# Windowed attention and a maxout feed-forward: first transfers per head half, x moved by DMA in the last three blocks, the first chunk masked by TensorE, half of the second products copied by ScalarE

## The chip, the core and the metric

The kernel runs on one NeuronCore of a Trainium2 chip. A core has TensorE (PE) for matrix products, VectorE (DVE), ScalarE (ACT) and GpSimd (POOL) for elementwise work, SyncE (SP) which here only issues transfers, and 16 DMA engines that move data between HBM and the on-chip memory SBUF. TensorE writes its products into PSUM, eight banks of 2 KB per partition, from which VectorE or ScalarE must fetch them. Each engine works through its own instructions in the order in which they were written; semaphores tie the engines together. The metric is the device time of one execution in microseconds.

## The reference

Four sequences of 768 positions, eight heads of 64, attend to the last 128 positions and to the first four (the sinks). The result, laid out as 3072 tokens of 512 features, goes through three products of which the elementwise maximum is kept, and an output product.

```python
scores = scale * np.matmul(q, k.transpose(0, 1, 3, 2))
is_sink = pos[None, :] < int(n_sink)
rel = pos[:, None] - pos[None, :]
keep = is_sink | ((rel >= 0) & (rel < int(window)))
...
a = np.exp(scores - max)
a = a / (np.sum(a, axis=-1, keepdims=True) + 1e-09)
attn = np.matmul(a, v)
...
x = attn.transpose(0, 2, 1, 3).reshape(B * S, H * D)
h = np.maximum(np.maximum(x @ w1, x @ w2), x @ w3)
out = h @ w_out
```

q, k, v are 4x8x768x64, w1 to w3 are 512x768, w_out is 768x512, all fp32 in HBM; products are made in bf16.

## The kernel before, in words

The 3072 tokens are 24 tiles of 128. Two tiles of one sequence are a chunk (12 chunks, `ch`, three to a sequence: c = 0, 1, 2), and the eight heads are taken as two halves of four (`g`). A unit is one chunk of one half: 24 units. Tiles are gathered in blocks (`BLOCKS`, L683: 2, 2, 4, 4, 4, 4, 4 tiles); a block's x goes through the feed-forward together.

**One unit** (`unit`, L382). q and k arrive by `qk_chunk` (L183): a GpSimd transfer which turns fp32 into bf16, into one of `NBUF` = 4 buffers per half. VectorE transposes them in pieces of 32x32 (L302). Scores (S, L412) are made with keys on the partitions, four heads at once in four row groups of TensorE, into `st`, which takes four of the eight PSUM banks and has one buffer only: the next unit's scores can start when this one's exps have read it. ScalarE takes the exp (E, L417), VectorE multiplies by a mask of zeros and ones (M, L424), TensorE multiplies by v, which has a column of ones for the denominator (PV, L433 and L442), VectorE divides (N, L452 and L461), TensorE transposes x (XT, L471), ScalarE copies it to `xT` (XC, L483). For c > 0 the sinks' scores are made apart (`sink_scores`) and multiplied by `vbd`, a block matrix of the sinks' v which SP fills by 16 small transfers per sequence (`sink_v`, L335).

**One block** (`block`, L548). For each of six blocks of 128 hidden features, three groups of four products (H, L562); ScalarE copies the first from PSUM to `h_sb` (L571), VectorE takes the maximum with the second and third (L573). Then for each tile six products with `wo_sb` (Y, L581), a copy by ScalarE (L588) and a store by SP (L595). H, Y, PV, XT and sink scores share the four other PSUM banks (`h_ring`).

**Loads.** `qk_first` (L162) brings q and k of chunk 0, half 0, as fp32 by SP and ScalarE, four transfers each, and ScalarE casts them (L306). GpSimd issues the rest in this order: q and k of half 1, the masks (`make_masks`), v of the first two tiles (`v_chunk`), a third of w1 to w3, the small constants `bd` and `ident`, chunk 1, two v tiles, the rest of w, chunk 2, two v tiles, `wo`. For later sequences, v comes as two large transfers (`v_batch`, L286) into one of two buffers (`vbufs`), issued between the first chunk's half 0 and half 1. Eight GpSimd transfers can be out at once.

**The order of everything** is worked out ahead of time by a list planner. Each piece of work is a `Task` with an engine, an assumed cost, the tasks it needs, a due time `want` and the buffers it takes; `arrange` (L41) picks, for each engine, among the 64 tasks due first, the one that could begin earliest. Each engine then gets its instructions in that order. `LEAD` makes a block's attention end some us before the block's turn. The planner only sets the order; on the chip each instruction waits for what it needs.

The softmax here doesn't subtract the row's maximum and nothing guards it: scores larger than these inputs give would overflow.

## Time and profile before

| | |
|---|---|
| median of 13 executions | 195.96 us (194.45 to 199.07) |
| the profiled execution | 196.5 us, of which 194.8 are the span from first to last instruction |
| instructions | 4237 |
| products H, 512 and 256 columns | L562: 345 and 144 seen, 379 and 285 ns each, 104.8 us busy |
| products Y | L581: 138 seen, 32.6 us busy |
| maxima of 128x512 from PSUM | L573: 60, 687 ns |
| masks of 128x1024 | L424: 40, 682 ns |
| exps of 128x1024 | L417: 40, 1023 ns |
| transposes of q and k | L302: 24 and 24, 633 and 626 ns |
| x to xT by ScalarE | L483: 24, 588 ns |
| HBM read and written | 25.17 MB, 6.29 MB |

The time is that of the device, the span lies inside it. Durations of one instruction are longer than the spacing in a pipelined series (two transposes of q and k start 0.46 us apart), and a few records of matmuls are missing: 489 of 504 H products are in the trace. A row of the timeline gives start, length, engine, line, operation, output and inputs, a count, and in brackets the idle time before it with what ended it.

### The profile page before, as it was taken

The page shows a single profiled execution, that of the slowest core. Times are in us where ns is not written, and L with a number is a line of the kernel's source. Part 1 is how long each engine was busy: PE and PEld are TensorE (multiplying, and loading weights), DVE is VectorE, ACT ScalarE, POOL GpSimd, SP SyncE. Part 2 cuts the span into 40 slices and gives each one's busy share as a digit, 9 for nine tenths or more (in the row PEclk, how much of TensorE's full clock was granted, in tenths as well). Part 3 has the DMA queues.
Part 4 walks back from the last instruction along what each step waited for, and adds up shares of the span by engine and source line. Part 5 has one row for each costly group of instructions (what it writes and reads, how often), then busy time and mean ns, then how long its engine had stood idle before and what let it go on. Part 6 is the DMA issues. An engine that isn't in the chain of part 4 may idle for free.

```text
span 194.8 us, 4237 instructions
## 1 busy us (share of the span) xinstructions
PE 168.3 (86%) x1659; PEld 94.7 (49%) x1680; DVE 128.8 (66%) x289; ACT 95.6 (49%) x147; POOL 55.5 (29%) x83
## 2 busy tenths in 40 slices
PE   0067988596799879999999999999999999999992
PEld 0044666265574445654445644555545556444440
DVE  4358676674999299996599953987906588035520
ACT  3253653672564616865266373827852572432222
POOL 7996758624692150257210000000000000000000
PEclk9999999999999999999999999999999999999999
DMA  5999999999999969099990022000050000230014
GB/s 110 130 155 163 195 188 176 175 140 216 137 129 137 145 67 177 25 88 179 238 140 13 3 108 111 0 0 3 0 204 15 2 3 0 108 113 0 0 54 162
DMA packets 58964, 19.52 MB, mean 100 GB/s; under 512 B 44352, under 2 KB 55616, under 8 KB 58944
## 3 DMA queue, kind: packets, MB, share of 16 engines
q0 software_dynamic: 54592, 12.40, 72.1%
q1 hardware_dynamic: 4160, 6.59, 9.5%
q10 hardware_dynamic: 192, 0.26, 0.5%
q8 instruction: 13, 0.21, 0.4%
q14 instruction: 7, 0.06, 0.1%
HBM read 25.17 MB, written 6.29 MB: 161 GB/s over the span
## 4 chain that ended last, share of the span: by engine, by line
PE 49%; DMA 28%; issue 10%; POOL 8%; SPq 2%; DVE 1%; ACT 0%; POOLq 0%; ACTq 0%
PE h L562 30%; DMA q_raw<-in_q_dram 14%; PE y L581 11%; DMA k_raw<-in_k_dram 7%; DMA v_sb<-in_v_dram 5%; PE o L442 3%; PE st L412 3%; POOL w_sb L199 3%; SPq L335 2%; PE xt L471 2%; POOL v_sb L290 2%; DMA vbd<-v_sb 1%; PE o L433 1%; POOL v_sb L194 1%; POOL q_raw L188 1%
## 5 line engine op out<-in xcount | busy, mean ns | idle before, releaser
L562 PE MATMUL h<-xT,w_sb 128*128 128x512 bf16 (+1 forms) x489 | 104.8, 351 | 5.4 <-DVE h_sb L573 3.7
L573 DVE TENSOR_TENSOR h_sb<-h,h_sb 128x512 bf16<-128x512 f32 (+1 forms) x84 | 51.2, 610 | 34.8 <-PE h L562 31.4
L562 PEld LDWEIGHTS <-w_sb 128*128 128x128 bf16 x504 | 46.1, 99 | 40.9 <-issue 4.1
L417 ACT ACTIVATE e_sb<-st 128x1024 bf16<-128x1024 f32 (+1 forms) x48 | 44.0, 952 | 17.1 <-PE st L412 16.3
L571 ACT CAST h_sb<-h 128x512 bf16<-128x512 f32 (+1 forms) x42 | 22.1, 526 | 43.7 <-PE h L562 43.5
L581 PE MATMUL y<-wo_sb,h_sb 128*128 128x512 bf16 x138 | 32.6, 379 | 2.1 <-DMA wo_sb<-in_moe_w_out_dram 1.8
L424 DVE TENSOR_TENSOR e_sb<-e_sb,mask 128x1024 bf16<-128x1024 bf16 (+1 forms) x48 | 29.7, 638 | 2.5 <-ACT e_sb L417 2.4
L412 PE MATMUL st<-qT,kT 32*128 32x128 bf16 (+1 forms) x512 | 15.4, 248 | 10.3 <-DVE kT L302 10.0
L302 DVE STREAM_TRANSPOSE qT<-q_raw 128x256 f32<-128x256 f32 x24 | 15.0, 633 | 13.5 <-DMA q_raw<-in_q_dram 13.5
L588 ACT COPY y_sb<-y 128x512 f32<-128x512 f32 x24 | 14.1, 587 | 16.4 <-PE y L581 14.0
L581 PEld LDWEIGHTS <-h_sb 128*128 128x128 bf16 x144 | 13.7, 98 | 17.0 <-issue 1.8
L461 DVE TENSOR_TENSOR x<-o,rc 128x256 bf16<-128x256 f32 x48 | 20.4, 424 | 1.8
L442 PEld LDWEIGHTS <-e_sb 128*128 128x128 bf16 x352 | 16.9, 99 | 8.2 <-DVE e_sb L424 2.5
L442 PE MATMUL o<-v_sb,e_sb 128*128 128x65 bf16 x352 | 18.9, 197 | 1.6 <-DVE e_sb L424 1.4
L483 ACT COPY xT<-xt 128x512 bf16<-128x512 bf16 x24 | 14.1, 588 | 12.5 <-PE xt L471 12.3
L188 POOL DMA_DIRECT2D k_raw<-in_k_dram x23 | 15.6, 676 | 14.0 <-DMA q_raw<-in_q_dram 7.8
L188 POOL DMA_DIRECT2D q_raw<-in_q_dram x23 | 15.9, 690 | 12.2 <-DMA q_raw<-in_q_dram 4.4
L412 PEld LDWEIGHTS <-kT 32*128 32x128 bf16 x512 | 10.2, 96 | 15.5 <-DVE kT L302 10.0
L302 DVE STREAM_TRANSPOSE kT<-k_raw 128x256 f32<-128x256 f32 x24 | 14.7, 626 | 1.2 <-DMA k_raw<-in_k_dram 1.2
L471 PE MATMUL xt<-ident,x 128*128 128x128 bf16 x96 | 12.3, 227 | 2.1 <-DVE x L461 2.1
L471 PEld LDWEIGHTS <-x 128*128 128x128 bf16 x96 | 7.6, 99 | 9.8 <-DVE x L461 4.4
L290 POOL DMA_DIRECT2D v_sb<-in_v_dram x6 | 8.6, 1442 | 12.5 <-PE st L412 10.5
(34 smaller groups left out, 48.1 us busy)
## 6 DMA issues: line engine op xcount, KB each, us to landing
out_dram<-y_sb SPq DMA_DIRECT2D x24, 256.0 KB
q_raw<-in_q_dram POOLq DMA_DIRECT2D x23, 128.0 KB, 9.9
k_raw<-in_k_dram POOLq DMA_DIRECT2D x23, 128.0 KB, 8.3
w_sb<-in_moe_w_dram POOLq DMA_DIRECT2D x9, 256.0 KB, 7.8
v_sb<-in_v_dram POOLq DMA_DIRECT2D x6, 384.0 KB, 10.8
vbd<-v_sb SPq DMA_DIRECT2D x64, 0.5 KB
v_sb<-in_v_dram POOLq DMA_DIRECT2D x6, 128.0 KB, 7.6
wo_sb<-in_moe_w_out_dram POOLq DMA_DIRECT2D x1, 768.0 KB, 9.3
```

Source lines behind the costliest of these rows:

```text
L188: nc.gpsimd.dma_start(out=raw(nm, ch, g), in_=s)
L302: nc.vector.transpose(dst, src)
L412: nc.tensor.matmul(ps[:, i, col:col + n], lhsT=kk[r, k0:k0 + 128, e], rhs=qT[r, q0:q0 + n, e], start=(e == 0), stop=(e == 1))
L417: nc.scalar.activation(st["e"][:, :, cols(tt)], st["ps"][:, :, cols(tt)], AF.Exp, scale=scale)
L424: nc.vector.tensor_tensor(out=ee, in0=ee, in1=m.unsqueeze(1).to_broadcast(list(ee.shape)), op=ALU.mult)
L442: nc.tensor.matmul(o[:, i, :], lhsT=st["e"][:, i, col:col + 128], rhs=vbufs[b % 2][:, 4 * g + i, kb, :], start=(c == 0 and n == 0), stop=( ...
L461: nc.vector.tensor_tensor(out=x, in0=o[:, :, :D], in1=rc.unsqueeze(2).to_broadcast([128, 4, D]), op=ALU.mult)
L471: nc.tensor.transpose(st["xt"][:, n, 128 * tt:128 * tt + 128], x[:, 128 * n:128 * n + 128], ident)
L562: nc.tensor.matmul(ps[:, :ntok], lhsT=w_sb[:, wi, d, fb * 128:fb * 128 + 128], rhs=xTs[blk][:, d, :ntok], start=(d == 0), stop=(d == DSUB ...
L571: nc.scalar.copy(hs, ps[:, :ntok])
L573: nc.vector.tensor_tensor(out=hs, in0=ps[:, :ntok], in1=hs, op=ALU.max)
L581: nc.tensor.matmul(ps, lhsT=box["h"][:, fb, 128 * m:128 * m + 128], rhs=wo_sb[:, fb, :], start=(fb == 0), stop=(fb == FSUB - 1))
```

## The change

- **Planner**: engines' clocks start at 0.8, 200 tasks are looked at instead of 64, and the assumed costs of loads are other ones.
- **Loads**: q of half 1 of chunk 0 comes as fp32 by SP too, with a cast by ScalarE; k of half 1 comes in four transfers by GpSimd. `NBUF` is 8, there are four v buffers, one per sequence, and v comes tile by tile for all sequences, after the q and k of both halves of its chunk.
- **Masks**: made from one triangle (`make_own`, GpSimd) by VectorE. For chunk 0 (`N_BY_PE` = 1) the mask is added before the exp: TensorE multiplies `ident` by a tile of zeros and -30000 into the score banks ahead of the scores, and VectorE's mask product falls away.
- **q's order**: q is transposed with the tokens of a tile in another order (j outside, m inside). For x that goes by TensorE, the copy to `xT` puts them back, in one copy per tile; for x that goes by DMA, the store to HBM does.
- **x by DMA** in blocks 5 to 7 (`FIRST_BY_DMA` = 5): x of both halves is gathered in `xd`, and SP issues one transposing transfer of 128x512 per tile into `xT` instead of XT and XC.
- **TWO**: in blocks 1 to 4, for hidden blocks 0, 2 and 4, ScalarE copies the second product to `h2`, and VectorE takes the maximum of two bf16 tiles in SBUF.
- **Blocks**: 2, 2, 2, 4, 4, 4, 4, 2 tiles; `LEAD` is 5.

```diff
-    clock = dict.fromkeys(engines, 0.0)
+    clock = dict.fromkeys(engines, 0.8)
...
-            for t in q[:64]:
+            for t in q[:200]:
...
+    if N_BY_PE:
+        neg = const.tile([128, 256], BF16, name="neg")
+        neg0 = const.tile([128, 384], BF16, name="neg0")
...
-    vbufs = [const.tile([128, H, 6, D + 1], BF16, name=f"v_sb{n}") for n in range(2)]
+    vbufs = [const.tile([128, H, 6, D + 1], BF16, name=f"v_sb{n}") for n in range(B)]
...
-    rate = 0.40
-
-    def load(name, mb, want, f, eng="POOL", cost=0.65, deps=(), lat=2.5):
+    rate = 0.38
+
...
-        dma_done[name] = task("DMA", mb / rate, lambda: None, deps=[t], want=want, lat=lat, name=name)
+        dma_done[name] = task("DMA", mb / (0.235 if name[0] == "v" else rate), lambda: None, deps=[t], want=want, lat=lat, name=name)
...
-    NBUF = 4
+    NBUF = 8
...
+    def qk_first(nm, src, g, e):
+
+        def f():
+            to = raw(nm, 0, g) if e is nc.gpsimd else first[nm, g]
+            for i in range(4):
+                e.dma_start(out=to[32 * i:32 * i + 32, :], in_=rows(src, 0, g)[i])
+        return f
...
+    def v_tile(b, n):
         def f():
-            s = v[0].rearrange("h (n p) d -> p n h d", p=128)
-            nc.gpsimd.dma_start(out=vbufs[0][:, :, n, :D], in_=s[:, n])
+            s = v[b].rearrange("h (n p) d -> p n h d", p=128)
+            nc.gpsimd.dma_start(out=vbufs[b][:, :, n, :D], in_=s[:, n])
...
+    load("q0.1", 0.26, -1999, qk_first("q", q, 1, nc.sync), eng="SP", cost=1.8)
...
+    def v_loads(ch):
+        b, c = divmod(ch, NC)
         for n in (2 * c, 2 * c + 1):
-            load(f"v0{n}", 0.26, nxt(), v_chunk(n), cost=0.9)
+            load(f"v{b}{n}", 0.26, nxt(), v_tile(b, n), cost=0.9)
...
+    def make_own():
+        nc.gpsimd.memset(mask[:, 128:], 1.0)
+        own = mask[:, 128:].rearrange("k (j m) -> k j m", j=8)
+        nc.gpsimd.affine_select(out=own, in_=own, compare_op=ALU.is_ge, fill=0.0,
+                                base=0, pattern=[[1, 8], [8, 16]], channel_multiplier=-1)
...
+        nc.vector.tensor_scalar(out=mask[:, :128], in0=mask[:, 128:], scalar1=-1.0, scalar2=1.0,
+                                op0=ALU.mult, op1=ALU.add)
+        nc.vector.tensor_copy(mask0[:, 0:128], mask[:, 128:256])
+        nc.vector.tensor_copy(mask0[:, 128:384], mask)
+        nc.vector.memset(mask0[0:n_sink, 0:256], 1.0)
+
+    def make_negs():
+        for m, n in ((mask, neg), (mask0, neg0)):
+            nc.vector.tensor_scalar(out=n, in0=m, scalar1=-1.0, scalar2=30000.0, op0=ALU.add, op1=ALU.mult)
...
+    load("k0.1", 0.26, nxt(), qk_first("k", k, 1, nc.gpsimd), cost=2.4)
+    for _ in range(3):
+        lanes.append(lanes[-1])
+    t_own = task("POOL", 1.8, make_own, want=nxt(), name="own")
+    t_ident = task("POOL", 0.6, make_ident, want=nxt(), name="ident")
...
+                src = raw(nm, ch, g).bitcast(F32)
+                dst = tile_T(nm, ch, g).rearrange("p s e -> p (s e)").bitcast(F32)
+                if nm == "q":
+                    dst = dst.rearrange("p (s j m) -> p j s m", s=2, j=8)
+                    src = src.rearrange("p (j s m) -> p j s m", j=8, s=2)
+                else:
+                    dst = dst.rearrange("p (m j) -> p j m", j=8)
+                    src = src.rearrange("p (j c) -> p j c", j=8)
...
+        by_pe = ch < N_BY_PE
...
+            if by_pe:
+                lo, hi = cols(tts[0]).start, cols(tts[-1]).stop
+                m = neg0[:, lo - 128:hi - 128] if c == 0 else \
+                    neg.unsqueeze(1).to_broadcast([128, len(tts), 256])
+                for i in range(4):
+                    nc.tensor.matmul(ps[:, i, lo:hi], lhsT=ident, rhs=m, start=True, stop=False,
+                                     skip_group_check=True)
...
-            src = st["xt"][:, :, 128 * tts[0]:128 * tts[0] + n]
-            nc.scalar.copy(xT_tile()[:, 2 * g:2 * g + 2, off:off + n], src)
+
+            src = st["xt"][:, :, 128 * tts[0]:128 * tts[0] + n].rearrange("p n (s j m) -> p n s m j", j=8, m=16)
+            dst = xT_tile()[:, 2 * g:2 * g + 2, off:off + n].rearrange("p n (s m j) -> p n s m j", j=8, m=16)
+            for t in range(len(tts)):
+                nc.scalar.copy(dst[:, :, t], src[:, :, t])
...
-        ms = {tt: task("DVE", 0.1 + n_e[tt] / 1880, masks(tt), deps=[es[tt], t_mask],
-                       want=w0 + (1.3 + 0.4 * tt) * dw, name=f"M{nm}{tt}") for tt in tts}
+        ms = es if by_pe else {
+            tt: task("DVE", 0.1 + n_e[tt] / 1880, masks(tt), deps=[es[tt], t_mask],
+                     want=w0 + (1.3 + 0.4 * tt) * dw, name=f"M{nm}{tt}") for tt in tts}
...
+                elif wi == 1 and fb in two:
+                    box["h2"] = ffn.tile([128, 512], BF16, name="h2", tag="h2", bufs=2)
+                    nc.scalar.copy(box["h2"][:, :ntok], ps[:, :ntok])
...
+        def both(fb):
+            def f():
+                hs = box["h"][:, fb, :ntok]
+                nc.vector.tensor_tensor(out=hs, in0=hs, in1=box["h2"][:, :ntok], op=ALU.max)
...
-                nc.sync.dma_start(out=out[r:r + 128, :], in_=box["ysb", m])
+                to = out[r:r + 128, :]
+                if blk >= FIRST_BY_DMA:
+                    to = to.rearrange("(m j) d -> j m d", j=8)
+                nc.sync.dma_start(out=to, in_=box["ysb", m])
...
-BLOCKS = [[0, 1], [2, 3], [4, 5, 6, 7], [8, 9, 10, 11], [12, 13, 14, 15], [16, 17, 18, 19], [20, 21, 22, 23]]
-TWO = ()
-LEAD = 6.0
+BLOCKS = [[0, 1], [2, 3], [4, 5], [6, 7, 8, 9], [10, 11, 12, 13], [14, 15, 16, 17], [18, 19, 20, 21], [22, 23]]
+TWO = {1: (0, 2, 4), 2: (0, 2, 4), 3: (0, 2, 4), 4: (0, 2, 4)}
+LEAD = 5.0
 N0 = 1
-N_BY_PE = 0
-FIRST_BY_DMA = 99
-XLAT = 3.0
+N_BY_PE = 1
+FIRST_BY_DMA = 5
+XLAT = 2.2
```

The transposing transfer was in the kernel before, unused, and is called now:

```python
        def xt_dma(tt):
            def f():
                o = off + 128 * (tt - tts[0])
                nc.sync.dma_start_transpose(out=xT_tile()[:, :, o:o + 128],
                                            in_=xs_tiles[ch, tt].rearrange("p h d -> p (h d)"))
            return f
```

## Prediction

> **What bounds the kernel now.** I read the page's busy rows and 40 slices first, then its chain.
>
> ```profile
> PE 168.3 (86%) x1659; PEld 94.7 (49%) x1680; DVE 128.8 (66%) x289; ACT 95.6 (49%) x147; POOL 55.5 (29%) x83
> ...
> PE   0067988596799879999999999999999999999992
> ...
> DMA  5999999999999969099990022000050000230014
> ...
> PE 49%; DMA 28%; issue 10%; POOL 8%; SPq 2%; DVE 1%; ACT 0%; POOLq 0%; ACTq 0%
> ```
>
> A slice is 4.87 us. From slice 20 (97 us) TensorE is at 9 everywhere and DMA mostly idle; before it DMA is at 9 and TensorE has 5s, 6s and 8s. So there are two regimes: an early half in which data arrives late, a later half bound by TensorE. DMA's 28% of the chain lies wholly in the first.
>
> Busy is not useful work, so I price TensorE by the steadiest rows of its chain: 47 products of 512 columns in 10.14 us, 0.216 each; 8 of 256 columns in 0.87, 0.109 each; 24 score products in 0.57 (16 in 0.46); 8 of value in 0.25; a transpose 0.055; a sink group 0.34. Before has 360+144 products of 512 columns (108.9 us), 144 of 256 (15.7), 16 score groups of 24 and 8 of 16 (12.8), 352 value products and 32 sink products at 0.11 (14.6), 96 transposes (5.3), five sink groups (1.7): **159 us** in a span of 194.8. The other 36 us are what a change can win; the timeline of TensorE shows where they are.
>
> ```profile
> 9.97 0.83 PE L412 MATMUL st<-qT,kT 32*128 32x256 bf16 x16 [9.97 <-DVE kT L302]
> ...
> 18.59 1.04 PE L412 MATMUL st<-qT,kT 32*128 32x128 bf16 x24
> ...
> 24.12 0.64 PE L412 MATMUL st<-qT,kT 32*128 32x128 bf16 x24
> ...
> 37.68 2.75 PE L581 MATMUL y<-wo_sb,h_sb 128*128 128x512 bf16 x11 [1.80 <-DMA wo_sb<-in_moe_w_out_dram]
> ...
> 49.76 0.60 PE L562 MATMUL h<-xT,w_sb 128*128 128x256 bf16 x4 [2.39 <-DVE h_sb L573]
> ...
> 58.06 2.75 PE L581 MATMUL y<-wo_sb,h_sb 128*128 128x512 bf16 x12
> ...
> 68.67 0.27 PE L433 MATMUL o<-vbd,e_sink 128*128 128x260 bf16 x1 [1.20 <-DVE h_sb L573]
> ```
>
> Counting work along the program's order: 14.8 us of it before the first output product (37.68), 30.7 before block 1's (58.06), 128.2 from there to TensorE's end at 191.25. **Loss: 22.9, then 4.5, then 5.0 us; 3.5 us of tail.** The stalls named h_sb at 49.76 and 68.67 are not the evacuation's fault: VectorE takes its instructions in order, and stood at a q or k transpose whose transfer was out.
>
> ```profile
> DVE qT L302 <- DMA q_raw<-in_q_dram: 13.5, 7, 4.1
> ```
>
> **The change, part by part.**
>
> *Loads.* Bytes stay. What moves is order. Before, batch 1's whole v (two issues, 31.5 to 34.4 us) sits between head half 0 and half 1 of chunk 3; k of half 1 is issued at 35.12 and lands 13.7 us later (48.8). After, all four q/k of a chunk come first, then two v tiles. Chunk 3's first half landed near 40.5; 0.5 MB of fp32 follows at about 0.3 MB/us (some 11 of the page's 25.2 MB are read by the time wo is in, 37.6): whole by about 42, its first v tile by 43.5. A chunk is then 1.6 MB, 5.2 us of transfer against 13 us of TensorE work (159/12). With eight raw buffers and four v buffers nothing on POOL waits for a consumer as it did for 10.5 us at 81. POOL issues 61 us in all (88 transfers at 0.67 to 0.91), spread over some 85: no bound. I take off the 2.39 us at 49.76 and, after 58.06, the stalls 1.20, 0.58 and 0.47 (68.67, 69.78, 97.60): 4.6 us.
>
> *Start.* Casts ran at 6.76 and 7.29. VectorE now takes q and k of half 0 only (two transposes, 0.46 apart), so first scores can begin near 8.6 instead of 9.97. q of half 1 comes on SP behind four issues of 0.45 (landing about 8.5), k in four POOL issues of 0.67 (same), which put v and w off by about 0.5 us; the two shorter POOL tasks give that back by the time of chunk 1. VectorE's six new mask steps, each no dearer than POOL's 0.24 to 0.39 for them now, end near 6.5, before the casts do.
>
> *First chunk masked by TensorE.* Removes four VectorE products (0.42+0.68 twice); adds eight matmuls of 384 columns. The first four run before the transposes. The second four stand in the path: the scores have one buffer, so they start only when the exps have read it. Here the rule is weighed against the row: the Trainium skill, "TensorE: Matmul & The Clock Gate", Part 1, says the clock doubles after about 3.4 us of sustained activity. By it, four would cost 4x0.16=0.64. But the timeline's 24 score products take 1.04 us at 18.59, 8.6 us after the first matmul, and 0.64 at 24.12, though the page's granted clock reads 9 throughout; activity with holes stays slow. I take 4x0.32=1.3 against 0.68 of mask saved: +0.6. Start and masks together: 1.4-0.6, first FFN product 0.8 us earlier.
>
> *Order of blocks.* Block sizes go from 2,2,4,4,4,4,4 tiles to 2,2,2,4,4,4,4,2. 256-column products take half as long, so work is the same (93.6 us both ways). What matters is the new order: the compiled TensorE order has 32 products of block 1 before the first output product, 19.6 us of work (masks 1.3 included) where before had 14.8. So **the 1.80 us for wo and the thin work around it get filled**. The feed doesn't move: chunk 2's last transposes end near 34.4 as now; then 24 FFN products, a score group and four more (2.6+0.6+0.4) put the first output product at 38.0, with 4.8 us more behind it. That is worth 4.8-1.3-0.3=3.2 us.
>
> *x by DMA in blocks 5 to 7.* Removes 40 transposes (2.2 us of TensorE) and 10 copies of 0.59 on ACT. Adds ten 128x512 transposing transfers on SP: none in the trace. The order leaves, between a block's last value products and its first FFN product, 24 output products (5.2 us) plus in two blocks a score group or more: 5.2 to 6.1 us. Lower end: SP's nearest row, SBUF to SBUF (issue 0.58, landing 2.67):
>
> ```profile
> 62.58 0.58 SPq L335
> ...
> 67.61 2.67 DMA vbd<-v_sb
> ```
>
> normalising 1.1 + two issues 1.2 + 2.7 = 5.0: no stall. Upper end: if the crossbar writes 32-byte pieces, each like those 130-byte packets (18.5 ns in the packet records), a transfer takes 4096x18.5/16 = 4.7 us, two in a row 9.4, stall about 7 us in each of three blocks. The nearest row has the same route; I take 1.0 in all. Behind the waiting SP instruction stand only stores, four y buffers deep.
>
> *Sink copies.* Batch 1's 16 vbd copies start when its first v tile lands (43.5) and take 11 us on SP, plus 2.67: 57.2. The order wants them at about 37.6-28.5=9 us of work after block 1's output, near 57.5. On the edge: 0.5 us. (Before, they ended at 70.3.)
>
> *ACT and VectorE.* Twelve second products copied by ACT: 6x0.37+6x0.59=5.8 us more; x copies come in two halves (0.37 twice for 0.59) for 14 units, +2.1, less the 5.9 saved. VectorE saves 6x(0.69-0.42), by the mask row of 128x512 bf16, and little on the 256-wide ones: some 2 us, plus shorter q steps. Both stay near 54 and 67% of the span. These hide beside TensorE; ACT's in-order queue also carries the exps, so I charge 0.5.
>
> *Tail.* Stores of the last blocks have an outermost dimension of 8. The Trainium skill, "DMA: Bandwidth & Descriptors", section "Why a DMA increments its semaphore by 16 and not by 1", lets a transfer use at most as many engines as divide that dimension. The last chain row
>
> ```profile
> 191.28 0.59 ACT y_sb L588
> ```
>
> ends 2.9 us before the span does, with 16 engines. By the row alone nothing changes; by the rule 256 KB on 8 engines of 27 GB/s takes 1.2 instead of 0.6 us. This rule speaks against the change and the store is exposed, so I take +0.7: tail 4.2.
>
> **Sum.** First output product 38.0 with 19.6 done. Work to block 1's output 10.1 (29.7 in the new order), loss 0.8: 48.9. Total new work 159-2.2+1.3=158.1; remaining 128.4. Loss: 5.0-2.25=2.75 as before, plus 1.0 transfers, 0.5 sinks, 0.5 ACT: 4.75. TensorE ends at 182.0; tail 4.2; **span 186.2**. The profiled execution took 196.5, 1.7 over its span: 187.9. It lay 0.5 over the median of 195.96, so I forecast **187.5 us**.
>
> **Rivals.**
> 1. *The early order gives nothing* (0.14): block 1's products wait for its x, or ACT with its copies holds the exps. For: 22.9 us are lost there through short chains of scores, exp, value and copy. Against: block 1's x depends on chunk 1, in by 20 us. The 3.2 us go, ACT costs 1 more: 191.7.
> 2. *Better than forecast* (0.14): the cold start warms earlier by the mask products, VectorE's shorter q steps and masks remove half the remaining losses. 3 to 5 us less: 183.5.
> 3. *Transposing transfers land late* (0.13, **slower**). Place: first FFN product of blocks 5, 6 and 7. For: no row shows one; cover is 6 us, and full TensorE leaves no slack. Decides from a stall of 3.2 us in each (9.5/3, the gain and the 1.0 charged), which is a last landing 9.3 us after the value products, or about 2.7 us per transfer. At 4.7 us each: 187.5+20=207.
> 4. *The parts cancel* (0.04): a middle landing, within 0.3% (about what measurement can tell) of 196.
>
> Forecast 0.55, between 184.5 and 191. Chances: faster 0.82, same 0.04, slower 0.14. The range 181.5 to 195 holds forecast and rivals 1 and 2, and leaves rival 3 out.
>
> **What would show it.** k of chunk 3 landing by 43; no DMA named before VectorE's transposes after 45; first output product near 38 without a wait for wo; block 1's near 49; TensorE at 9 from then on; first FFN product of blocks 5 to 7 with under 1 us of wait; last copy to end of span over 3 us. Wrong if the first FFN product of block 5 waits for xT over 3 us, or if slices up to 10 still show 5s and 6s.

## The result and the profile after

| | before | forecast | after |
|---|---|---|---|
| median | 196.21 us (48 executions) | 187.5 us | 193.07 us (11 executions, 191.36 to 197.14) |
| ratio of after to before, 95% interval | | 0.957 | 0.983 [0.979, 0.987] |
| profiled execution | 196.5 us | 187.9 us | 192.22 us |
| span | 194.8 us | 186.2 us | 190.49 us |
| first output product of the first block | 37.7 | 38.0 | 37.8 |
| first output product of the second block | 58.1 | 48.9 | 48.9 |
| TensorE's end | 191.25 | 182.0 | 184.34 |
| from there to the end of the span | 3.5 | 4.2 | 6.15 |

The change makes the kernel faster, by 1.7% where 4.3% were forecast. Single executions of one kernel lie 1 to 2% around its median, so the comparisons below are ratios with intervals, and the profiles serve to show where time goes; one profiled execution may lie a few us off its kernel's median.

The page of the changed kernel first: busy totals, the TensorE and DMA rows of the 40 slices (here 4.76 us each), and the shares of the chain that ended last.

```profile
PE 165.9 (87%) x1700; PEld 98.7 (52%) x1720; DVE 124.6 (65%) x305; ACT 96.8 (51%) x170; POOL 63.1 (33%) x93
...
PE   0487796899987979999989999999999999999960
...
DMA  5999999999999999999991011250050440014403
...
PE 61%; DMA 24%; POOL 6%; issue 3%; DVE 2%; ACT 1%; ACTq 0%; DVEq 0%; POOLq 0%
```

TensorE's share of the chain rose from 49 to 61%. Slices 7 to 10 read 8, 9, 9, 9, where before they read 5, 9, 6, 7; but slice 12 (57 to 62 us) and slice 14 (67 to 71 us), counted from 0, hold 7s, and the last one reads 0. The TensorE timeline gives the places.

```profile
37.81 2.76 PE L616 MATMUL y<-wo_sb,h_sb 128*128 128x512 bf16 x11 [0.51 <-DMA wo_sb<-in_moe_w_out_dram]
...
48.87 2.75 PE L616 MATMUL y<-wo_sb,h_sb 128*128 128x512 bf16 x11
...
55.72 0.60 PE L588 MATMUL h<-xT,w_sb 128*128 128x256 bf16 x4 [0.92 <-DVE h_sb L602]
...
61.97 0.29 PE L495 MATMUL xt<-ident,x 128*128 128x128 bf16 x2 [1.20 <-DVE x L485]
...
69.53 0.28 PE L466 MATMUL o<-v_sb,e_sb 128*128 128x65 bf16 x4 [1.06 <-issue]
...
70.13 2.75 PE L616 MATMUL y<-wo_sb,h_sb 128*128 128x512 bf16 x11
```

The first two milestones fall within 0.2 us of the forecast; a wait of 0.51 us for `wo` is left, where the forecast had none. Then it takes 21.3 us (48.87 to 70.13) until the third block's output, with waits for VectorE at 55.72 and 61.97, and a wait of 1.06 at 69.53 for which the profile names no releaser. VectorE's own timeline says what it stood at. The maximum that TensorE waits for at 55.72 (the first of those at 55.25) and the division that it waits for at 61.97 (the one at 61.49) both stand a few instructions behind a transpose of q that waited for its transfer.

```profile
53.62 0.77 DVE L317 STREAM_TRANSPOSE qT<-q_raw 128x256 f32<-128x256 f32 x2 [2.20 <-DMA q_raw<-in_q_dram]
...
55.25 1.28 DVE L602 TENSOR_TENSOR h_sb<-h,h_sb 128x256 bf16<-128x256 f32 x3
...
60.94 0.45 DVE L317 STREAM_TRANSPOSE qT<-q_raw 128x256 f32<-128x256 f32 x1 [0.71 <-DMA q_raw<-in_q_dram]
...
61.49 0.42 DVE L485 TENSOR_TENSOR x<-o,rc 128x256 bf16<-128x256 f32 x1
```

The chain of waits over the same stretch, in order of time (start, length, what), is loads up to 60.94 us:

```profile
40.87 10.56 DMA v_sb<-in_v_dram
...
51.71 9.21 DMA q_raw<-in_q_dram
...
60.94 0.45 DVE qT L317
```

That is the same kind of loss which the forecast had seen in before at 49.76 and 68.67 and had written off. At the other end, ScalarE's last copy of y begins at

```profile
184.40 0.59 ACT y_sb L623
```

so the span runs on for 5.50 us after it ends (190.49 - 184.99), against 2.93 in before (194.80 - 191.87).

The theory to test: two terms of the sum failed, each by about 2 us of span. **Loads**: q of later chunks still lands after VectorE has reached its transpose, because the planner believes in a faster supply than the chip gives. **Tail**: the last stores cost far more than 0.7 us. Rivals: VectorE is simply too full between 49 and 70 us (17.0 of 21.3 us busy); the small v transfers are what makes the supply slow; the products masked by TensorE or ScalarE's copies cost more than was charged.

### The profile page after: what moved, and what is told of

It is laid out like the page before. It is cut to its first block, busy times and chain, and to the rows that moved or that the text cites. A ratio compares the mean times of both kernels' runs of the same rounds, so it can differ in the third digit from the quotient of the medians.

```text
span 190.5 us, 4372 instructions
## 1 busy us (share of the span) xinstructions
PE 165.9 (87%) x1700; PEld 98.7 (52%) x1720; DVE 124.6 (65%) x305; ACT 96.8 (51%) x170; POOL 63.1 (33%) x93
## 4 chain that ended last, share of the span: by engine, by line
PE 61%; DMA 24%; POOL 6%; issue 3%; DVE 2%; ACT 1%; ACTq 0%; DVEq 0%; POOLq 0%
PE h L588 37%; DMA q_raw<-in_q_dram 14%; PE y L616 14%; DMA v_sb<-in_v_dram 6%; DMA w_sb<-in_moe_w_dram 5%; PE st L435 4%; PE o L466 4%; POOL w_sb L204 2%; PE o L457 1%; POOL k_raw L183 1%; PE xt L495 1%; POOL v_sb L199 1%; DVE x L485 1%; ACT y_sb L623 0%; DVE h_sb L602 0%
## 5 line engine op out<-in xcount | busy, mean ns | idle before, releaser
L588 PE MATMUL h<-xT,w_sb 128*128 128x256 bf16 (+1 forms) x564 | 103.1, 325 | 5.0 <-ACT xT L510 1.9
L588 PEld LDWEIGHTS <-w_sb 128*128 128x128 bf16 x576 | 52.5, 98 | 38.2 <-issue 4.3
L602 DVE TENSOR_TENSOR h_sb<-h,h_sb 128x256 bf16<-128x256 f32 (+1 forms) x84 | 46.3, 555 | 27.8 <-PE h L588 16.4
L597 ACT CAST h_sb<-h 128x256 bf16<-128x256 f32 (+1 forms) x48 | 23.3, 485 | 37.7 <-PE h L588 35.7
L199 POOL DMA_DIRECT2D v_sb<-in_v_dram x24 | 21.8, 909 | 5.5 <-DMA q_raw<-in_q_dram 2.9
L317 DVE STREAM_TRANSPOSE qT<-q_raw 128x256 f32<-128x256 f32 x24 | 10.0, 427 | 6.7 <-DMA q_raw<-in_q_dram 5.2
L510 ACT COPY xT<-xt 128x256 bf16<-128x256 bf16 x28 | 9.1, 381 | 9.3 <-PE xt L495 9.2
L485 DVE TENSOR_TENSOR x<-o,rc 128x256 bf16<-128x256 f32 x28 | 11.9, 424 | 1.0
L476 DVE RECIPROCAL rc<-o 128x4 f32<-128x4 f32 x48 | 8.3, 173 | 4.7 <-PE o L466 4.7
L495 PE MATMUL xt<-ident,x 128*128 128x128 bf16 x56 | 7.0, 223 | 3.0 <-DVE x L485 3.0
```

What stands on the lines that cost most here:

```text
L199: nc.gpsimd.dma_start(out=vbufs[b][:, :, n, :D], in_=s[:, n])
L317: nc.vector.transpose(dst, src)
L588: nc.tensor.matmul(ps[:, :ntok], lhsT=w_sb[:, wi, d, fb * 128:fb * 128 + 128], rhs=xTs[blk][:, d, :ntok], start=(d == 0), stop=(d == DSUB ...
L597: nc.scalar.copy(hs, ps[:, :ntok])
L602: nc.vector.tensor_tensor(out=hs, in0=ps[:, :ntok], in1=hs, op=ALU.max)
```

## The experiments

All ratios are to the kernel before, run on the same chip. The third column, from the profile, is when the first output product of the third block (block 2 in the kernel's count, the second being block 1) begins: the place where the forecast and the changed kernel part.

| run | ratio [95%] | third block's output at, us | last copy to end of span, us |
|---|---|---|---|
| the change, as it is | 0.983 [0.979, 0.987] | 70.1 | 5.50 |
| the change again | 0.976 [0.971, 0.982] | 70.0 | 5.50 |
| loads alone | 1.012 [1.008, 1.017] | 84.9 (a block of four tiles) | 3.19 |
| loads and blocks | 0.981 [0.975, 0.986] | 68.6 | 3.17 |
| no x by DMA | 0.983 [0.977, 0.989] | 69.9 | 3.19 |
| no mask by TensorE | 0.988 [0.982, 0.993] | 69.7 | 5.50 |
| no copies by ScalarE | 0.978 [0.970, 0.985] | 68.5 | 5.44 |
| no late loads | 0.965 [0.959, 0.972] | 66.8 | 5.3 |
| masks of two chunks left out | 0.990 [0.981, 0.999] | 70.4 | 5.5 |
| v in two large transfers | 0.987 [0.978, 0.996] | 69.2 | 5.5 |
| plain stores | 0.966 [0.958, 0.974] | 69.0 | 3.09 |
| order in h, strided writes | 1.004 [0.996, 1.012] | 69.5 | 3.09 |
| order in h, strided reads | 0.976 [0.969, 0.984] | 69.8 | 3.09 |
| measured rates alone | 0.964 [0.959, 0.969] | 66.8 | 5.29 |
| measured rates and strided reads | **0.954 [0.947, 0.961]** | 66.4 | 3.09 |
| the same without copies by ScalarE | 0.958 [0.953, 0.963] | 66.3 | 3.09 |

**The change again.** No edit; it sets the scale for the runs on its chip.

> The changed kernel as it is, so that the others have their base on the same chip. Every theory: a ratio to before near 0.983 and a span near 190.5 us, with some 5.5 us from the end of the last copy of y to the end of the span.

The third block's output and the tail repeat to 0.2 us, so both losses belong to the kernel and not to one execution. The ratio, 0.976, is within 0.7% of the first comparison; differences below about 1% between chips are not read here.

### Which part brings the gain

**Loads alone.** The changed loads, buffers and planner, with the old blocks and none of the other parts.

```diff
-BLOCKS = [[0, 1], [2, 3], [4, 5], [6, 7, 8, 9], ..., [22, 23]]
-TWO = {1: (0, 2, 4), 2: (0, 2, 4), 3: (0, 2, 4), 4: (0, 2, 4)}
-LEAD = 5.0
+BLOCKS = [[0, 1], [2, 3], [4, 5, 6, 7], ..., [20, 21, 22, 23]]
+TWO = {}
+LEAD = 6.0
-N_BY_PE = 1
-FIRST_BY_DMA = 5
+N_BY_PE = 0
+FIRST_BY_DMA = 99
```

> The changed kernel's loads, buffers, planner numbers, q order and masks made by VectorE, with before's blocks and without the three other parts (mask by TensorE, x by DMA, copies by ScalarE). If the gain comes from the loads' order and buffers: block 1's output starts 4 us or more earlier than before's 58.1 and the ratio is near 0.985. If the block sizes and the order that they allow bring it: under 0.5% from before, with block 1's output within 2 us of 58.1.

Measured 1.012 [1.008, 1.017]: no faster than before, although the second block's output came early as the theory wanted. Its TensorE timeline, by the output products of the second and third block and the waits between them (the view ends at 85 us and cuts the last row):

```profile
52.21 2.75 PE L616 MATMUL y<-wo_sb,h_sb 128*128 128x512 bf16 x12
...
62.77 1.02 PE L588 MATMUL h<-xT,w_sb 128*128 128x512 bf16 x4 [2.47 <-DVE h_sb L602]
...
68.19 0.27 PE L457 MATMUL o<-vbd,e_sink 128*128 128x260 bf16 x1 [3.12 <-DVE h_sb L602]
...
84.86 0.39 PE L616 MATMUL y<-wo_sb,h_sb 128*128 128x512 bf16 x1
```

and what VectorE stood at:

```profile
61.23 0.45 DVE L317 STREAM_TRANSPOSE qT<-q_raw 128x256 f32<-128x256 f32 x1 [3.24 <-DMA q_raw<-in_q_dram]
...
67.11 0.45 DVE L317 STREAM_TRANSPOSE qT<-q_raw 128x256 f32<-128x256 f32 x1 [2.91 <-DMA q_raw<-in_q_dram]
```

The second block's output comes 5.9 us earlier than in before (58.1), and all of it is gone by the third (84.9; before 84.6): in between VectorE waits for q for 6.9 us (the two waits above and 0.78 at 53.62), where before waited once (3.45 us at 67.46). Work done early was worth nothing here, since the next load set the pace.

**Loads and blocks.** The changed loads and block sizes; the other three parts off (`TWO = {}`, `N_BY_PE = 0`, `FIRST_BY_DMA = 99`).

> The changed kernel's loads, buffers, planner and block sizes; without the mask by TensorE, without copies of the second product by ScalarE and without x by DMA. Theory: the smaller third block is what turns the new loads into an early gain. Against the loads alone (197.6 us) it wins the 3.2 us of the forecast: first output product near 38, block 1's near 49, and 193 to 195 us. Rival: the gain needs the mask by TensorE or the copies, and the blocks alone stay at 197 us or more.

Measured 0.981 [0.975, 0.986]: against the loads alone, the block sizes and `LEAD`, which changed together, win 3% by these two ratios. Output begins at 37.8, 48.5 and 68.6. Behind the third block's output the profile shows no wait of TensorE with the loads alone and one of 0.83 us here, so the gain lies ahead of it; that it is the smaller third block and not `LEAD` is likely, and not shown. This run has the whole gain of the change: mask by TensorE, x by DMA and ScalarE's copies together move the ratio by nothing that can be told (0.983 and 0.976 with them), though each moves time inside.

**No x by DMA** (`FIRST_BY_DMA = 99` in the changed kernel).

> The changed kernel with x by TensorE in all blocks: 40 transposes and 10 x copies come back, the transposing transfers and the stores on half of the engines go. Theory: 2.2 us more of TensorE in a stage that it bounds, 2.6 us less of tail, within 0.7 us of the changed kernel. Rival (the transposing transfers cost time where no wait shows): over 1.5 us less.

The ratio is 0.983 [0.977, 0.989], against 0.976 [0.971, 0.982] for the change on the same chip; the intervals overlap. Inside there are two opposite terms. The tail is 2.3 us shorter, and TensorE waits here twice for ScalarE's copies of x:

```profile
102.21 4.91 PE L588 MATMUL h<-xT,w_sb 128*128 128x512 bf16 x22 [2.94 <-ACT xT L510]
...
179.54 7.80 PE L588 MATMUL h<-xT,w_sb 128*128 128x256 bf16 x70 [0.83 <-ACT xT L510]
```

The second wait belongs to x by TensorE. From the product at 102.21 to TensorE's end it takes 87.7 us here and, from the same product, 84.4 us in both executions of the change. The 3.3 us are the 40 transposes (2.2), this wait of 0.83, and 0.3 for which no row is shown.

The first wait does not belong to it. It is for the x of block 4, which TensorE moves in both kernels, and the change has it too (0.90 us; 1.52 in the repeated run). Kernels that move x by DMA had 2.39 (plain stores), 2.80 (order in h, strided reads) and 3.68 (no mask by TensorE). SP's queue offers an explanation; from the repeated run, SP, ScalarE and TensorE:

```profile
85.21 10.40 SPq L350 DMA_DIRECT2D vbd<-v_sb  x16
95.82 4.29 SPq L633 DMA_DIRECT2D out_dram<-y_sb  x5
...
99.16 0.59 ACT L623 COPY y_sb<-y 128x512 f32<-128x512 f32 x1 [2.46 <-DMA out_dram<-y_sb]
...
100.35 4.91 PE L588 MATMUL h<-xT,w_sb 128*128 128x512 bf16 x22 [1.52 <-ACT xT L510]
```

The 16 sink copies of the last sequence begin when chunk 9's last v tile has landed (85.3 us, packet records) and hold SP until 95.6. A store of block 2 stands behind them and keeps one of the four y buffers, so ScalarE's fourth copy of block 3 finds no free buffer, and the copy of x behind it is late. In the runs with loads and blocks, without copies by ScalarE and with measured rates, that store is issued ahead of the sink copies (77.5 to 78.5 us), and the wait is gone. It is gone too without late loads, where the sink copies end at 79.7. No run tests this alone.

**No mask by TensorE** (`N_BY_PE = 0`).

> The changed kernel with the first chunk masked by VectorE. The prediction's charge (four cold mask products stand in the path): the first FFN product comes 0.6 us earlier than the changed kernel's 15.6. Rival (the mask products are hidden, and start the clock's warming): it comes 0.5 us or more later, and the first block's products run slow for longer. Time within 0.5 us either way.

The first FFN product begins at 14.86 instead of 15.57 us, so the mask by TensorE costs 0.7 us there. The output products of the first two blocks begin at 38.0 and 49.0, as with it: until `wo` is in, 0.7 us are not seen. The ratio, 0.988 [0.982, 0.993], shows no gain from leaving it out.

**No copies by ScalarE** (`TWO = {}`).

> The changed kernel without the twelve second products copied by ScalarE. The prediction's charge: 0.5 us faster. Rival (VectorE is short in the stretch of block 2, and saves 0.14 us in each of three products there and 0.27 in block 3 and 4): the stretch gets longer by up to 1 us. Supply theory: nothing over 0.5 us either way while data is late.

The third block's output begins at 68.5 instead of 70.1, but the fourth's no earlier than in the change (92.4 and 92.2). The last copy ends 1.1 us earlier (183.92), about what the wait for the x of block 4 cost, which this order does not have. So the copies by ScalarE, or the order that comes with them, cost about 1 us of span; in the ratio, 0.978 [0.970, 0.985], that is not resolved.

### What makes the third block late

**No late loads.** This kernel leaves out the q and k transfers of chunks 5 to 11; their transposes read older data.

```diff
+        ch = ch if ch < 5 else 2 + ch % 3
...
-            nc.gpsimd.dma_start(out=raw(nm, ch, g), in_=rows(src, ch, g))
+            if ch < 5:
+                nc.gpsimd.dma_start(out=raw(nm, ch, g), in_=rows(src, ch, g))
```

> The changed kernel, order of instructions kept, but the q and k loads of chunks 5 to 11 are left out (those chunks read the tiles of chunks 2 to 4). Supply theory (in block 2's stage, VectorE stands in order at transposes whose transfers are out): the stretch from block 1's first output product to block 2's, 21.3 us in the changed kernel, falls by 2 to 4 us, VectorE's waits for q (2.2 and 0.7 us) go, and the time falls by as much. Rival (VectorE is full there whatever arrives): the stretch stays within 1 us.

The third block's output comes at 66.8 instead of 70.1 us, 17.9 us after the second's instead of 21.3, with the same instructions in the same order on TensorE and VectorE, and the ratio is 0.965 [0.959, 0.972]. VectorE has the same work there: being full was not the reason. The packet records add that v tiles, now alone, land 1.0 us apart.

**Masks of two chunks left out.** The mask products of chunks 4 and 5 are not made, which takes work off VectorE in this stretch.

```diff
         def masks(tt):
             def f():
+                if ch in (4, 5):
+                    return
```

> The changed kernel, order kept, but the mask products of chunks 4 and 5 are left out: eight VectorE products, 5 us of its work in the same stretch. Theory that VectorE is full there: the stretch falls by 3 us or more. Supply theory: under 1.5 us, since the transfers are as late as before.

The third block's output came no sooner (70.4), but from a late start: the first block's was at 40.1 in this execution, 2.3 us later than in the change. The stretch took 19.3 us, 2.0 less than in the change, which lies between the two expectations; other kernels that reached the second block's output late have it as short with all masks (19.0 and 19.3 with the order in h). VectorE still waited 2.33 us for q in it, and the ratio, 0.990 [0.981, 0.999], is no better than the change's. So less work for VectorE didn't remove the wait, and beyond that this run decides nothing.

**v in two large transfers**, per sequence from 1 on, after the q and k of the sequence's first chunk.

```diff
         for n in (2 * c, 2 * c + 1):
-            load(f"v{b}{n}", 0.26, nxt(), v_tile(b, n), cost=0.9)
+            if b == 0:
+                load(f"v{b}{n}", 0.26, nxt(), v_tile(b, n), cost=0.9)
+        if b and c == 0:
+            for hf in range(2):
+                load(f"v{b}h{hf}", 0.79, nxt(), v_batch(b, hf), cost=1.4)
```

> The changed kernel, but v of sequences 1 to 3 comes in two large transfers again, after q and k of the first chunk. If small v transfers are what makes the supply slow (about 7 us per chunk between 40 and 90 us, where before took about 1 us per v tile inside a batch and 0.8 per q or k), v tiles land about 1 us apart, later chunks' q and k come earlier, and the stretch shortens. If order is what matters, the batch stands ahead of chunk 4's q and k and the stretch gets longer by 2 us or more.

The expected stretch did not get longer (20.8 us); the loss came one block later. VectorE's waits for q grew to 11.0 us in all, 5.50 of them at 92.43, and the fourth block's output came 30.8 us after the third's (22.1 in the change). The last q and k land at 97.8 us, against 95.9 in the change (packet records). So larger v transfers do not speed up the supply.

**Measured rates alone.** The planner's two numbers for the supply are replaced by what the packet records of the changed kernel show; nothing else.

```diff
+    def mb_per_us(name):
+        if name[0] == "v":
+            return 0.16 if int(name[1]) else 0.235
+        late = name[0] in "qk" and int(name[1:].split(".")[0]) >= 3
+        return 0.27 if late else rate
...
-        dma_done[name] = task("DMA", mb / (0.235 if name[0] == "v" else rate), ...
+        dma_done[name] = task("DMA", mb / mb_per_us(name), ...
```

> The changed kernel with one edit alone: the planner is told the supply that its trace shows (v of sequences 1 to 3 at 0.16 MB/us instead of 0.235, q and k from chunk 3 on at 0.27 instead of 0.38). Stores stay as the change has them. Theory: the assumed rates put the q transposes of chunks 5 and 6 too early in VectorE's order, so this edit alone takes the stretch from the first output product of block 1 to that of block 2 from 21.2 to 17.1 us as in the version with both edits, TensorE's last output product ends near 180, and the tail of 5.5 us stays: about 188.5 us, ratio 0.96. Rival: the gain of both edits together (0.954) is mostly the tail, and the rates move work that comes back later: above 190.5 us, ratio over 0.97.

0.964 [0.959, 0.969], median 188.55 us. The transfers come no sooner than in the changed kernel (the last of q and k lands at 98 us against 96, by the packet records), and the instructions are the same ones. What differs is their order, on VectorE and with it on the others; VectorE's timeline:

```profile
52.28 0.44 DVE L323 STREAM_TRANSPOSE qT<-q_raw 128x256 f32<-128x256 f32 x1
...
54.04 0.42 DVE L608 TENSOR_TENSOR h_sb<-h,h_sb 128x256 bf16<-128x256 f32 x1
...
67.27 0.44 DVE L323 STREAM_TRANSPOSE qT<-q_raw 128x256 f32<-128x256 f32 x1
```

One q, not two, is transposed at 52.28, without a wait; another stands at 67.27, behind the divisions and maxima and not among them. On TensorE the third block's output begins here, with no wait over 0.3 us since the second's:

```profile
49.58 2.75 PE L622 MATMUL y<-wo_sb,h_sb 128*128 128x512 bf16 x11
...
60.89 0.60 PE L594 MATMUL h<-xT,w_sb 128*128 128x256 bf16 x4 [0.27 <-DVE h_sb L608]
...
66.84 2.54 PE L622 MATMUL y<-wo_sb,h_sb 128*128 128x512 bf16 x11
```

That is 17.3 us instead of 21.3. In this stretch VectorE no longer waits for q at all, where it waited 2.91 us in the change. Over the whole span its waits for q are longer than in the change, 6.1 us against 5.2, but they lie elsewhere (3.61 us at 18.36, 1.38 at 95.54), and TensorE shows no wait at the later one. What counts is where VectorE waits and what stands behind it. The rival lost: the ratio is that of the theory (0.96), and the tail, 5.29 us, stayed.

### What makes the tail long

**Plain stores.** The blocks from 5 on store their rows straight, which permutes the rows of the output.

```diff
                 to = out[r:r + 128, :]
-                if blk >= FIRST_BY_DMA:
-                    to = to.rearrange("(m j) d -> j m d", j=8)
```

> The changed kernel, but blocks 5 to 7 store their rows as block 0 does (128 rows outermost), so the rows of these blocks come out in the permuted order. Theory (the tail is the store on half of the engines): the time from the last copy to the end of the span falls from 5.5 to about 2.9 us, as before, and the time by about 2.6 us (1.3%). Rival (the tail is the latency of a last transfer, whatever its shape): under 0.5 us.

From the last copy to the end of the span 3.09 us instead of 5.50, so the form of the store costs 2.4 us there. The ratio is 0.966 against 0.976 for the change on the same chip, with intervals that overlap slightly; it agrees with the 2.4 us and does not measure them. The packet records say how it comes about: a plain store's 128 packets of 2 KB are written within 0.83 us in before, and each store is over before the next begins. In the changed kernel the last two stores run from 184.96 to 189.12 as one train of 4.16 us, 2.1 each; a packet takes 118 ns instead of 85, and 256 x 118 ns in 4.16 us are 7.3 packets at a time, against 128 x 85 ns in 0.83, 13. That fits eight engines instead of sixteen; the records do not name the engine.

**Order in h, strided writes.** For the last block alone, the order is put back when `h_sb` is written, and its stores are plain.

```diff
+                if blk == len(BLOCKS) - 1:
+                    hs = hs.rearrange("p (s m j) -> p s j m", m=16, j=8)
+                    src = ps[:, :ntok].rearrange("p (s j m) -> p s j m", m=16, j=8)
...
-                if blk >= FIRST_BY_DMA:
+                if FIRST_BY_DMA <= blk < len(BLOCKS) - 1:
```

> The changed kernel, but the last block puts its tokens back in order when it fetches its products from PSUM, so its two stores have 128 rows outermost. Tail theory: as the plain store, 2.6 us less, if ScalarE and VectorE hide their strided writes (they are busy 3.3 and 5.1 of 10.5 us there). Rival (strided writes of 2-byte values are slow): under 1 us less, or slower.

The tail shrinks to 3.09 and the kernel is no faster than before (1.004). The groups by shape, from 150 us on: the copy (L600) and the maximum (L602) of the last block in this kernel,

```profile
L602 DVE TENSOR_TENSOR h_sb<-h,h_sb 128x256 bf16<-128x256 f32 x11 | 13.5, 1399 | 6.5 <-ACT h_sb L600 6.0
...
L600 ACT CAST h_sb<-h 128x256 bf16<-128x256 f32 x6 | 7.7, 1304 | 5.9 <-PE h L588 5.9
```

and with the sides exchanged (next run):

```profile
L602 DVE TENSOR_TENSOR h_sb<-h,h_sb 128x256 bf16<-128x256 f32 x12 | 5.1, 425 | 7.5 <-ACT h_sb L600 5.1 <-PE h L588 1.8
...
L600 ACT CAST h_sb<-h 128x256 bf16<-128x256 f32 x6 | 2.2, 373 | 4.6 <-PE h L588 4.6
```

The number after the comma is the mean of one in ns. Writing bf16 values 16 bytes apart makes both instructions over three times slower. ScalarE's copy has only its output in that form; VectorE's maximum reads one input in it too.

**Order in h, strided reads.** As above, with both sides walked in the order `p s m j`: the reads from PSUM jump, the writes are contiguous.

> As the run which put the last block's tokens in order, but the strided side is now the read from PSUM and the write to SBUF is contiguous. If only strided 2-byte writes are slow (1.3 us instead of 0.37 measured), the fetches take what they take in the changed kernel, the last stores run on all engines and the time falls by 2.4 us (1.2%). If strided reads are slow too, it is again slower than the changed kernel.

Mean 373 and 425 ns, as without any reordering (374 and 425 in the changed kernel), and the tail is 3.09. The ratio, 0.976 [0.969, 0.984], overlaps with that of the change; the 2.4 us are seen in the span's end and, next, on top of the other mend.

### Both mends

**Measured rates and strided reads.** The two edits together.

> The changed kernel with the last block's order restored on the read, and with the planner told the measured supply (q and k from chunk 3 on at 0.27 MB/us instead of 0.38, v from sequence 1 on at 0.16 instead of 0.235: 7 us per chunk), so that it sets VectorE's transposes later. Supply theory: VectorE's waits for q at 53 and 61 us go, the stretch from block 1's to block 2's first output product falls from 21.2 by 2 to 3 us, the tail is 3.1 us, and the time is 4 to 5 us under the changed kernel's (ratio near 0.96). Rival (data is late whatever the order): the stretch stays and TensorE waits at the scores instead; 2.4 us for the tail alone (ratio near 0.97).

0.954 [0.947, 0.961], median 186.03 us, span 184.2: faster than either kernel. The gain over the change is 7.0 us by the medians, measured on different chips, more than the 4 to 5 expected: the stretch fell by 4.2 us (to 17.1), not by 2 to 3, the tail by 2.4, and the wait for the x of block 4 is gone. Against the rates alone the ratio is 1% lower, with intervals that overlap slightly. TensorE's row of slices is at 9 from slice 9 to the last but one, where the changed kernel's dips:

```profile
PE   0588896979999999999999999999999999999991
```

and its last copy,

```profile
180.53 0.58 ACT L637 COPY y_sb<-y 128x512 f32<-128x512 f32 x1 [0.71 <-PE y L630]
```

ends 3.09 us before the span does.

**The same without copies by ScalarE** (`TWO = {}`).

> The version with measured rates and the order put back in the read of PSUM, and besides with no second product copied by ScalarE. Theory: the copies by ScalarE add work to an in-order queue that also carries the exps, and VectorE, at 68% of the span, needs no relief, so it is no slower without them: 184.5 to 186.5 us. Rival: with the supply waits gone VectorE is fuller in blocks 1 to 4, and the copies pay: 188 us or more.

0.958 [0.953, 0.963], 186.91 us: between the two values expected and not to be told from the run with the copies. So they neither help nor hurt measurably here.

## Why the prediction fell short, step by step

- **Start and masks**: first FFN product forecast 0.8 us earlier, measured 1.6 (15.57 against 17.19), mostly because the first scores began at 8.03, not near 8.6. A 6 is left in slice 6 (29 to 33 us), which the forecast had named as a sign against it; it cost nothing further, for `wo` comes later still. The masks by TensorE cost 0.7, as charged (0.6): four products took 1.44 us at 10.46, as at 5.66, close to the 1.3 from the row of score products. The rule of the Trainium skill ("TensorE: Matmul & The Clock Gate", Part 1) gives 0.64, an estimate, only after some 3.4 us of sustained activity, and TensorE had been busy for 2.66 of the 4.80 us before; the row was the better guide. The gain is invisible afterwards, as the forecast said of the feed for the first output product.
- **Order of blocks**: 38.0 and 48.9 forecast, 37.8 and 48.9 measured. The first is partly luck: TensorE was ready at 37.3 and waited 0.51 us for `wo`, a wait that the forecast had taken as filled. The step held, and it carries the measured gain: with the loads it gives 0.981, the loads alone 1.012.
- **Loads**: this step failed. It took "5.2 us of transfer" for a chunk against 13 us of work, concluded that "nothing on POOL waits for a consumer", and took off the stalls at 49.76, 68.67, 69.78 and 97.60. A chunk's last v tile lands 6.9 us after that of the chunk before (42.7 for chunk 3 to 97.6 for chunk 11, in the packet records), 0.23 MB/us where 0.3 was taken from the time before 38 us. That is still faster than TensorE uses chunks up, and yet the stalls came back: VectorE is given the transposes in the order of the planner, which counted on 0.38 and 0.235 MB/us, so that they stood up to 2.20 us at q with maxima queued behind. "No DMA named before VectorE's transposes after 45" was the right test, and it failed. TensorE's end: 184.34 us instead of 182.0. From the second block's output on, TensorE lost 184.34 - 48.87 - 128.4 = 7.1 us instead of 4.75; with the measured rates, where its last product ends at 180.7, it lost 180.7 - 49.6 - 128.4 = 2.7. Of these 4.4 us, 4.0 lie in the stretch to the third block's output (21.3 against 17.3). The supply, in the planned order, and not the second block sets the third: in the runs with plain stores and with the order in h, the second block's output came 1.6 to 1.8 us later than in the change (50.5 to 50.6) and the third's no later (69.0 to 69.8).
- **x by DMA**: the charge of 1.0 for late transfers was too high. SP's pair of transposing transfers is issued in 2.51 us (below), eight of the ten are written in about 0.8 us each and the other two within 2.0 (512 packets of 256 bytes in the records, where rival 3 had assumed 4096 pieces and 4.7 us), and the first FFN product of blocks 5, 6 and 7 follows the output products with no wait at all. Rival 3, the slower side, had no footing. Its worth on TensorE was 3.3 us in this order, and not the 2.2 of the transposes alone.

```profile
120.11 5.35 PE L616 MATMUL y<-wo_sb,h_sb 128*128 128x512 bf16 x23
125.31 4.48 PE L588 MATMUL h<-xT,w_sb 128*128 128x512 bf16 x20
...
169.31 2.51 SPq L515 DMA_TRANSPOSE xT<-xd  x2
```

- **Sink copies and ACT**, 0.5 each: the sink copies of sequence 1, which the forecast had on the edge, left no wait for `vbd` before the third block's output. Those of the last sequence, which it did not look at, held a store and with it TensorE for 0.90 us at 99.89. ScalarE's copies cost about 1 us up to the last copy (184.99 against 183.92), that wait included, and nothing that the ratio shows. Of the lighter rivals, the first (the early order gives nothing) fell with the second block's output at 48.87.
- **Tail**: this step failed by its size. "+0.7" was worked out for one store on eight engines at full rate; the rule in "DMA: Bandwidth & Descriptors", section "Why a DMA increments its semaphore by 16 and not by 1", of the Trainium skill pointed the right way. Measured: +2.6 (from the last copy to the end 5.50 against 2.93). A store takes 2.1 us, longer than the 1.3 us between two copies, so the second last store holds up the last, whose packets begin at 187.23, 2.24 us after its copy has ended (0.85 in before).
- **Sum**: 186.2 of span forecast, 190.49 measured; TensorE's end gives 2.3 of the difference and the tail 1.95. The rest to the medians (193.07 - 187.5 = 5.6) is that this profiled execution lies 0.85 us below its median, where 0.4 above had been assumed.

Rival 4, that parts cancel, was right about two of them: most of what x by DMA gains on TensorE (3.3 us), its stores lose again at the end (2.3). Not settled is why a chunk takes 6.9 us when v tiles alone land 1.0 us apart; larger v transfers did not change it.

## What to carry to other kernels

A planner that fixes an in-order engine's order needs the rate that loads have in the stretch concerned, read from the trace of the kernel itself: too hopeful a rate puts a waiting instruction ahead of ready ones, and here correcting two numbers was worth more than the three cleverer parts of the change. An in-order queue that only issues transfers can also hold up the kernel: a store that stood behind sixteen small copies kept a buffer, and an engine waited for the buffer. Where a trick moves a permutation into the store, look at the last two stores and at the gap between them, because nothing hides those. When bf16 elements must be reordered on the way from PSUM to SBUF, let the reads jump and keep the writes contiguous, as was cheaper here.

## What the runs showed of the hardware

- A 128x256 copy from PSUM that writes bf16 with a stride of 16 bytes took 1304 ns on ScalarE, and a maximum that writes so and reads one input so took 1399 on VectorE, against 373 and 425 with the stride on the side of PSUM and 374 and 425 with none: the jump in the read cost nothing.
- A store of 128 rows of 2 KB with an outermost dimension of 8 took 2.1 us (the mean of the last two), against 0.83 plain.
- Two transposing transfers of 128x512 bf16 from SBUF to SBUF are issued in 2.51 us and written in about 0.8 us each (eight of the ten), and 5.2 us of output products covered them without a wait.
